# Two groups of heads at a time: kv in the off-diagonal blocks and M in four 64x64 quadrants

## The chip, the core and the metric

The kernel runs on one core of a Trainium2 chip. The core has a matrix engine (TensorE, in the profile PE, with its weight loads as PEld), VectorE (DVE), ScalarE (ACT), GpSimd (POOL), and SyncE (SP), whose queue issues all of this kernel's transfers in the order of the program. The metric is the device time of one execution in microseconds (us). Three runs of the kernel before gave 307.9, 307.93 and 309.0; their median is 307.93.

## The reference

Two blocks read the same input x (2048 rows of 640) and are mixed by a gate. Cut to what matters here:

```python
g = sigmoid((x * gate_w).sum(-1, keepdims=True))
a = A_ref(x, ...)                  # a state-space convolution, 640 channels
q, k, v = heads(x @ wqkv)          # 32 heads of 20
pq, pk = phi(q), phi(k)            # phi(t) = where(t > 0, t + 1, exp(t)) + 1e-6
kv = einsum("bhsd,bhse->bhde", pk, v)
z = einsum("bhsd->bhd", pk)
num = einsum("bhqd,bhde->bhqe", pq, kv)
den = einsum("bhqd,bhd->bhq", pq, z)[..., None] + 1e-6
b = (num / den) @ wo
return g * a + (1 - g) * b
```

kv is a 20x20 matrix for each head, so over all heads it is block diagonal, 640x640 with 32 blocks. The kernel never forms num: it multiplies kv by wo first, which gives one matrix M of 640x640, and the last stage is a product of the normalised pq with M.

## The kernel before

**Stages.** In the first stage (to about 147 us of the span) TensorE computes k for 16 row tiles and accumulates G, the product of x with phi(k), in PSUM. Since v = x @ wv, the matrix kv is Wv' G, cut to its blocks. Then comes the stage that the change is in, which mixes three things on TensorE: the q blocks (20 of them, five for each quarter of the rows; 15 matmuls of 128x128 by 512 columns each), the kv products and the M products. The last stage holds 20 final products, `fp`.

**Exactness.** Operands are split into a high and a low part (`hi` on ScalarE, `lo` on VectorE), and three matmuls give one product (`mm3`, L104 to L107). The kv and M products are instead plain fp32 matmuls, which the profile shows as two instructions for a call.

**Groups.** The 640 channels of the heads are cut into six groups of 120 (the last has 40). A group lies on the partitions in two parts of 60, from partition 0 and from 64 (`parts`, L250); the last group has one part of 40. `wo_load` (L254) loads the group's rows of wo in the same layout.

**kv of a group** (`kv_mm`, L261). For each of the five blocks b of 128 rows of G, and each part, one matmul of 128 rows by 60 weights by 60 columns; the parts write partitions 0 and 64 on of one PSUM bank of the tag `f` (three buffers). VectorE then multiplies each part with the block mask `bdm` and puts it into a diagonal block of `kvT`, a 128x128 tile in SBUF that was zeroed at the start. There are two such tiles, used in turn.

**M of a group** (`m_mm`, L271). One matmul for each half of 320 columns, with the 124x124 of `kvT` as weights and the group's rows of wo as the moving operand, into two banks of the tag `m` (two buffers). ScalarE writes the high part `Mgh`, VectorE the low part `Mgl`, for each half, and SP stores the parts to DRAM: four stores for a group, two for the last.

**Order.** The order of the stage is written out by hand in `PLAN` (L63): q is a q block, kv and m with a number are the products of that group, z and c are small steps (the gate's row, a block of the convolution), d the denominator of a quarter (`q_den`, L643), n the normalisation of a block (`q_norm`), ml the reload of M in another layout (`m_load`, L673, ten loads of 320 KB, followed by loads of u), y and f the steps of the last stage. Every engine runs its own instructions in this order; tags with a number of buffers say what waits for what. The q blocks' PSUM tag is `q` (three buffers); the denominator's product `dp` and the final products share the tag `f` with kv. The load of wo's last group waits for the buffer of group 3 and is issued behind m3 (L728).

Of the kernel before, what the change touches and what calls it, by code (L numbers as in the profile page):

```python
# [30 lines left out]
F32 = mybir.dt.float32  # L31
F32R = mybir.dt.float32r
I32 = mybir.dt.int32
AF = mybir.ActivationFunctionType
OP = mybir.AluOpType
# [4 lines left out]
P = 128  # L40
L = 2048
D = 640
NB = D // P
# [17 lines left out]


PLAN = """  # L63
q0 kv0 q0 z kv1 q0 m0 q0 m1 kv2 c q0 m2 kv3 
q1 m3 kv4 d0 q1 m4 kv5 n0 q1 n0 m5 ml n0 q1 n0 y q1 n0
q2 q2 y q2 d1 n1 f q2 n1 y f q2 n1 n1 f n1 f
q3 f q3 d2 n2 f q3 n2 f q3 n2 n2 f q3 n2 f
f d3 n3 f n3 n3 f n3 f n3 f
# [5 lines left out]
def f32(ap):  # L74
    return ap.bitcast(F32)


def body(tc, i, outT):
    nc = tc.nc
    pe, act, dve, pool, sp = nc.tensor, nc.scalar, nc.vector, nc.gpsimd, nc.sync  # L80
    outer, top, kst = ExitStack(), ExitStack(), ExitStack()

    def mk(stack, name, space=None):
        kw = {} if space is None else {"space": space}
        if space is not DRAM:
            kw["reuse_waits"] = "tile"
        return stack.enter_context(tc.tile_pool(name=name, bufs=1, **kw))
# [5 lines left out]
    pw = mk(top, "pw")  # L93
# [4 lines left out]
    def hi(dst, src):  # L98
        act.activation(dst, src, AF.Copy)  # L99

    def lo(dst, src, h, eng=None):
        (eng or dve).tensor_tensor(dst, src, f32(h), op=OP.subtract)  # L102
# [6 lines left out]
    def col(tag, n=NB, dt=F32):  # L109
        return pc.tile([P, n], dt, tag=tag, name=tag)  # L110
# [27 lines left out]
    bdm = col("bdm", HC)  # L138
    kvz = [col(f"kvT{k}", P) for k in range(2)]
# [7 lines left out]
    GT = pc.tile([P, NB, D], F32, tag="m1", name="GT")  # L147
    Wv = pc.tile([P, NB, D], F32, tag="m2", name="Wv")
    M_d = [dram.tile([D, D], F32, name=f"M_d{x}") for x in "hl"]
# [97 lines left out]
    kvs, wos = {}, {}  # L247


    def parts(gi):  # L250
        c0, n = GRP[gi]
        return [(r, c0 + o, min(HC, n - o)) for r, o in ((0, 0), (64, HC)) if o < n]
# [5 lines left out]
            m = min(64, D - c) if r == 0 else n  # L258
            sp.dma_start(w[r : r + m, :D], i["wo"][c : c + m, :])

    def kv_mm(gi):  # L261
        p = pqp.tile([P, 512], F32, tag="f", bufs=3, name="kvps")
        for b in range(NB):
            for r, c, n in parts(gi):
                pe.matmul(p[r : r + n, :n], Wv[:, b, c : c + n], GT[:, b, c : c + n],
                          start=(b == 0), stop=(b == NB - 1))
        kvT = kvs[gi] = kvz[gi % 2]
        for r, c, n in parts(gi):
            dve.tensor_tensor(kvT[r : r + n, r : r + n], p[r : r + n, :n], bdm[r : r + n, :n], op=OP.mult)

    def m_mm(gi):  # L271
        wo, kvT = wos.pop(gi), kvs.pop(gi)
        n = parts(gi)[-1][0] + parts(gi)[-1][2]
        ps = []
        for hf in range(2):
            ps.append(mbank("mps")[:n, :320])
            pe.matmul(ps[hf], kvT[:n, :n], wo[:n, hf * 320 : hf * 320 + 320], start=True, stop=True)  # L277
        h = pq.tile([P, D], F32R, tag="so", bufs=2, name="Mgh")
        l = pw.tile([P, D + 2], F32R, tag="st", bufs=3, name="Mgl")
        for hf in range(2):  # L280
            sl = slice(hf * 320, hf * 320 + 320)
            hi(h[:n, sl], ps[hf])
            lo(l[:n, sl], ps[hf], h[:n, sl])
        for v, to in ((h, M_d[0]), (l, M_d[1])):
            for r, c, m in parts(gi):
                sp.dma_start(to[c : c + m, :], f32(v[r : r + m, :D]))


    def gates():
# [5 lines left out]
    def gates_row():  # L295
        gp = mbank("gp")
        pe.transpose(gp[:NT, :P], g, ident)
        gr = pc.tile([NT, P], F32, tag="gr", name="gr")
        dve.tensor_copy(gr, gp[:NT, :P])
        sp.dma_start(g_d, gr)  # L300
        for gi in range(NG):
            gb_load(gi)
# [12 lines left out]
    def z_const():  # L315
        cp = mbank("cp")
        pe.matmul(cp[:, :2], bm, zsh, start=True, stop=False)
        pe.matmul(cp[:, :2], bm, zsl, start=False, stop=True)
        dve.tensor_scalar(ch, cp[:, :1], EPS, EPS, op0=OP.mult, op1=OP.add)
# [81 lines left out]
    def conv_out(j):  # L401
        y = conv(j)
        y_d[j] = dram.tile([P, 512], F32, name=f"y_d{j}")
        sp.dma_start(y_d[j], y)
# [190 lines left out]
    pq = mk(top, "pq")  # L595
    pqp = mk(top, "pqp", PSUM)

    def mbank(name):
        return pqp.tile([P, 512], F32, tag="m", bufs=2, name=name)

    def rem_out():
        for b0, b1 in ((0, 4), (4, NB)):
            tp = mbank("tp")
            for b in range(b0, b1):
                pe.transpose(tp[:, (b - b0) * P : (b - b0 + 1) * P], rem[:, b * P : b * P + P], ident)
            hi(GT[:, b0:b1, 512:], tp[:, : (b1 - b0) * P].rearrange("p (b s) -> p b s", s=P))
# [4 lines left out]
    def q_block(gi, b):  # L611

        qp = pqp.tile([P, 512], F32, tag="q", bufs=3, name="qp")
        w, o = (wqA, b * P) if b < 3 else (wqB, (b - 3) * P)
        for c in range(NB):
            mm3(qp, w[0][:, c, o : o + P], w[1][:, c, o : o + P], xTh[gi][:, c, :], xTl[gi][:, c, :],
                c == 0, c == NB - 1)
        if len(qe) + len(pend) == NE:
            flush()
        e = qe[gi, b] = pq.tile([P, 512], F32, tag="e", bufs=NE, name="qe")  # L620
        r = pq.tile([P, 512], F32, tag="r", bufs=2, name="qr")
        act.activation(e, qp, AF.Exp)  # L622
        act.activation(r, qp, AF.Relu)  # L623
        for h, _, v in pend:
            hi(h, v)
        dve.scalar_tensor_tensor(e, e, 1.0, r, op0=OP.min, op1=OP.add)  # L626
        if b == 0:
            a = acc[gi] = pq.tile([P, 512], F32, tag="acc", bufs=1, name="acc")
            act.activation(a, e, AF.Copy, scale=zc[:, :1])
        else:  # L630
            a = acc[gi]
            dve.scalar_tensor_tensor(a, e, zc[:, b : b + 1], a, op0=OP.mult, op1=OP.add)
        if b == NB - 1:
            ah = pq.tile([P, 512], F32R, tag="r", bufs=2, name="acch")
            al = pq.tile([P, 512], F32R, tag="accl", bufs=1, name="accl")
            hi(ah, a)
            lo(al, a, ah)
            acc[gi] = ah, al
        for h, l, v in pend:
            lo(l, v, h)  # L640
        pend.clear()

    def q_den(gi):  # L643

        dp = pqp.tile([P, 512], F32, tag="f", bufs=3, name="dp")
        ah, al = acc.pop(gi)
        pe.matmul(dp, bm, ah, start=True, stop=False)
        pe.matmul(dp, bm, al, start=False, stop=True)
        d = pq.tile([P, 512], F32, tag="d", bufs=1, name="d")
        act.activation(d, dp, AF.Identity, bias=ch)  # L650
        dve.reciprocal(d, d)
        o = pq.tile([P, 512], F32, tag="r", bufs=2, name="og")
        act.activation(o, gbs[gi], AF.Copy, bias=1.0, scale=-1.0)
        dve.tensor_tensor(d, d, o, op=OP.mult)
        rd[gi] = d

    def q_norm(gi, b):
        e = qe.pop((gi, b))
        if b == 0:
            pqT[gi] = [px.tile([P, NB, 512], F32R, tag=f"x{c}{gi}", name=f"pT{c}{gi}") for c in "hl"]  # L660
        h, l = [v[:, b, :] for v in pqT[gi]]
        dve.scalar_tensor_tensor(e, e, EPS, rd[gi], op0=OP.add, op1=OP.mult)  # L662
        flush()
        pend.append((h, l, e))
# [7 lines left out]
    m = {}  # L672
# [36 lines left out]
    for w in PLAN.split():  # L709
        what, k = w.rstrip("0123456789"), int("0" + w.lstrip("abcdefghijklmnopqrstuvwxyz"))  # L710
        if what == "q":
            q_block(*divmod(n_q, NB))
            n_q += 1
            if n_q == 1:
                rem_out()
        elif what == "z":
            z_const()
            gates_row()
        elif what == "d":
            q_den(k)  # L720
        elif what == "n":
            q_norm(*divmod(n_n, NB))
            n_n += 1
        elif what == "kv":
            kv_mm(k)
        elif what == "m":
            m_mm(k)
            if k == 3:  # L728
                wo_load(NB)
        elif what == "ml":  # L730
            m_load()
            for j in range(NS, min(NS + 3, NJ)):
                u_load(j)
        elif what == "c":
            conv_out(n_c)
            n_c += 1
            if n_c < NS:
                u_load(n_c)
        elif what == "y":
            y_block(n_y)  # L740
            n_y += 1
        elif what == "f":
            flush()
            final_mm(n_f)
            final_out(n_f)
            n_f += 1
            if n_y < NJ:
                y_block(n_y)
                n_y += 1
# [172 lines left out]
```

## Time and profile before

| | |
|---|---|
| median of three runs | 307.93 us (307.9 to 309.0) |
| profiled execution, its time | 308.53 us |
| its span, first to last instruction | 306.7 us |
| PE busy | 300.8 us, 98% of the span |
| DVE busy | 230.3 us, 75% |
| ACT busy | 118.5 us, 39% |
| POOL busy | 45.6 us, 15% |
| transfers | 45.98 MB, mean 150 GB/s |

The profile is of one execution. An engine's busy time leaves out what only waits or issues transfers. The chain of waits follows the work that ended last back from the last instruction; a piece of it has its start, its length, and the engine, tile and line. A timeline gives the instructions of one engine in order of time, equal neighbours merged (x4 is four of them), each with its start and duration; matmuls are pipelined, so the duration of one is longer than the distance to the next. A wait row reads: who waited, for whom, total us, times, longest.

### The profile page before, as it was taken

What the parts mean: (1) busy time and instruction counts of PE and PEld (TensorE: products, weight loads), DVE (VectorE), ACT (ScalarE), POOL (GpSimd) and SP (SyncE); (2) the same over time, 40 slices, a digit from 0 to 9 for tenths busy, and PEclk for the clock granted to TensorE, in tenths of its full rate; (3) what the DMA queues carried; (4) which work ended last, traced back from release to release, by engine and by line L of the source; (5) the groups of instructions that cost most, each with busy time, mean ns of one, the idle gap of its engine ahead of it and who ended that gap; (6) DMA issues with size and microseconds to landing.
All of it is one profiled execution on the core that took longest, in us unless ns stands there. A gap on an engine that the chain in (4) does not pass through costs nothing.

```text
span 306.7 us, 4494 instructions
## 1 busy us (share of the span) xinstructions
PE 300.8 (98%) x1607; PEld 259.2 (85%) x1607; DVE 230.3 (75%) x356; ACT 118.5 (39%) x249; POOL 45.6 (15%) x50
## 2 busy tenths in 40 slices
PE   8999999999999999999999999999999999999994
PEld 8998899999999999998887777888888888788884
DVE  2949976899899799937444768867684677788992
ACT  4455143453544534327335354553323223312200
POOL 3605340000000000000000000003223103241631
PEclk9999999999999999999999999999999999999999
DMA  6817285057767855380526352692315122244423
GB/s 190 296 65 223 84 245 175 35 190 226 236 161 234 255 166 174 102 268 0 158 86 219 119 170 94 196 344 79 121 50 166 42 68 68 68 139 141 134 104 108
DMA packets 28408, 45.98 MB, mean 150 GB/s; under 512 B 3771, under 2 KB 10827, under 8 KB 28383
## 3 DMA queue, kind: packets, MB, share of 16 engines
q1 hardware_dynamic: 28383, 45.66, 47.2%
q8 instruction: 14, 0.23, 0.3%
q14 instruction: 11, 0.09, 0.1%
HBM read 32.92 MB, written 12.72 MB: 149 GB/s over the span
## 4 chain that ended last, share of the span: by engine, by line
PE 94%; DVE 4%; issue 1%; ACT 0%; POOL 0%; DVEq 0%; POOLq 0%
PE qp L105 8%; PE fp L105 8%; PE fp L107 8%; PE qp L107 8%; PE qp L106 7%; PE fp L106 7%; PE k L107 6%; PE k L106 6%; PE k L105 6%; PE g L227 5%; PE g L224 5%; PE g L225 5%; PE g L430 4%; PE mps L277 2%; PE r L240 1%; PE r L238 1%
## 5 line engine op out<-in xcount | busy, mean ns | idle before, releaser
L415 POOL TENSOR_TENSOR yb<-yb,gb 128x512 f32<-128x512 f32 x20 | 28.5, 1432 | 225.7 <-DVE qe L626 162.9
L105 PE MATMUL fp<-pTh,Mh 128*128 128x512 f32 (+1 forms) x105 | 40.1, 382 | 0.6 <-DVE o L701 0.6
L107 PE MATMUL fp<-pTl,Mh 128*128 128x512 f32 (+1 forms) x105 | 40.2, 383 | 0.0
L106 PE MATMUL fp<-pTh,Ml 128*128 128x512 f32 (+1 forms) x105 | 40.0, 381 | 0.0
L626 DVE SCALAR_TENSOR_TENSOR qe<-qe,qr 128x512 f32<-128x512 f32 x20 | 14.8, 740 | 28.3 <-ACT qr L623 28.3
L224 PE MATMUL g<-ph,xh 128*128 128x512 f32 x80 | 31.6, 395 | 0.0
L225 PE MATMUL g<-ph,xl 128*128 128x512 f32 x80 | 31.5, 394 | 0.0
L199 ACT ACTIVATE e<-k 128x320 f32<-128x320 f32 x25 | 11.0, 439 | 51.5 <-PE k L107 51.5
L99 ACT ACTIVATE pTh<-qe 128x512 fp32r<-128x512 f32 x20 | 12.6, 633 | 39.3 <-DVE qe L662 39.3
L203 DVE SCALAR_TENSOR_TENSOR e<-e,r 128x320 f32<-128x320 f32 x32 | 16.2, 511 | 14.7 <-ACT r L200 14.6
L227 PE MATMUL g<-pl,xh 128*128 128x512 f32 x80 | 26.4, 394 | 0.1
L622 ACT ACTIVATE qe<-qp 128x512 f32<-128x512 f32 x20 | 12.0, 598 | 37.0 <-PE qp L107 34.6
L105 PE MATMUL qp<-xTh,wqAh 128*128 128x512 f32 x60 | 24.0, 400 | 0.0
L105 PEld LDWEIGHTS fp<-pTh,Mh 128*128 128x128 f32 x105 | 19.7, 188 | 4.9 <-DVE o L701 1.0
L107 PE MATMUL qp<-xTl,wqAh 128*128 128x512 f32 x60 | 23.6, 394 | 0.0
L106 PE MATMUL qp<-xTh,wqAl 128*128 128x512 f32 x60 | 23.6, 393 | 0.0
L106 PEld LDWEIGHTS fp<-pTh,Ml 128*128 128x128 f32 x105 | 19.7, 188 | 4.1
L107 PEld LDWEIGHTS fp<-pTl,Mh 128*128 128x128 f32 x105 | 19.8, 188 | 3.9
L395 DVE TENSOR_TENSOR_SCAN y<-y,cY,zero 128x512 f32<-128x512 f32 x16 | 20.5, 1279 | 0.9 <-ACT y L394 0.8
L102 DVE TENSOR_TENSOR pTl<-qe,pTh 128x512 fp32r<-128x512 f32 x20 | 16.0, 812 | 6.7 <-ACT pTh L99 6.3
L107 PE MATMUL k<-wkAl,xTh 128*128 128x322 f32 x60 | 19.0, 317 | 0.0
L106 PE MATMUL k<-wkAh,xTl 128*128 128x322 f32 x60 | 18.9, 315 | 0.0
(168 smaller groups left out, 725.6 us busy)
## 6 DMA issues: line engine op xcount, KB each, us to landing
xraw<-in_x SPq DMA_DIRECT2D x16, 320.0 KB, 4.8
u<-in_xT SPq DMA_DIRECT2D x20, 256.0 KB, 5.6
out_T<-o SPq DMA_DIRECT2D x19, 256.0 KB, 2.5
y_d<-y SPq DMA_DIRECT2D x16, 256.0 KB, 2.2
yb<-y_d SPq DMA_DIRECT2D x16, 256.0 KB, 3.2
xTraw<-in_xTt SPq DMA_DIRECT2D x12, 320.0 KB, 4.9
Wv<-in_wv SPq DMA_DIRECT2D x5, 320.0 KB, 6.8
Mh<-M_dh SPq DMA_DIRECT2D x5, 320.0 KB, 4.8
```

The lines of the kernel that those rows point to most:

```text
L99: act.activation(dst, src, AF.Copy)
L102: (eng or dve).tensor_tensor(dst, src, f32(h), op=OP.subtract)
L105: pe.matmul(out, ah, bh, start=start, stop=False)
L106: pe.matmul(out, al, bh, start=False, stop=False)
L107: pe.matmul(out, ah, bl, start=False, stop=stop)
L203: dve.scalar_tensor_tensor(e, e, 1.0, r[:, :n], op0=OP.min, op1=OP.add)
L224: pe.matmul(gps[b], xh[:, s], h[:, :512], start=t == 0, stop=False)
L225: pe.matmul(gps[b], xl[:, s], h[:, :512], start=False, stop=False)
L227: pe.matmul(gps[b], xh[:, b * P : b * P + P], l[:, :512], start=False, stop=t == NT - 1)
L395: dve.tensor_tensor_scan(y, y, zero.to_broadcast([P, 512]), cY[:, c], op0=OP.add, op1=OP.add)
L415: pool.tensor_tensor(ys[j], ys[j], gbs[j // NB], op=OP.mult)
L626: dve.scalar_tensor_tensor(e, e, 1.0, r, op0=OP.min, op1=OP.add)
```

## The change

Groups are taken in pairs (0 and 1, 2 and 3, 4 and 5). `kv_mm` makes the kv of both groups into one PSUM bank, the second group's in columns 64 on, with the same matmuls as before; VectorE puts the first group's two parts into the diagonal 64x64 blocks of `kvT` and the second group's into the off-diagonal ones (`out_row`: the second group's output rows change places). `m_mm` then makes one matmul for each 64x64 quadrant and half: a group's part reads 60 rows of partitions and writes 64 rows of PSUM, with its place in the array given. A half needs two banks, one for each group: the tag `m` for the first half, the tag `f` for the second. High and low parts and stores are as before, group after group, with 128 rows where it was 124. The load of wo's last group is issued behind the second pair's stores. `PLAN` has three kv and three m steps at other places, and ml follows the eighth q block where it followed the ninth.

```diff
 PLAN = """
-q0 kv0 q0 z kv1 q0 m0 q0 m1 kv2 c q0 m2 kv3 
-q1 m3 kv4 d0 q1 m4 kv5 n0 q1 n0 m5 ml n0 q1 n0 y q1 n0
+q0 kv0 q0 z q0 m0 kv1 q0 c q0 m1 kv2
+q1 d0 q1 m2 ml n0 q1 n0 n0 q1 n0 y q1 n0
...
-    def kv_mm(gi):
+    def out_row(gi, r):
+        return r if gi % 2 == 0 else 64 - r
+
+    def kv_mm(pr):
         p = pqp.tile([P, 512], F32, tag="f", bufs=3, name="kvps")
-        for b in range(NB):
-            for r, c, n in parts(gi):
-                pe.matmul(p[r : r + n, :n], Wv[:, b, c : c + n], GT[:, b, c : c + n],
-                          start=(b == 0), stop=(b == NB - 1))
-        kvT = kvs[gi] = kvz[gi % 2]
-        for r, c, n in parts(gi):
-            dve.tensor_tensor(kvT[r : r + n, r : r + n], p[r : r + n, :n], bdm[r : r + n, :n], op=OP.mult)
+        kvT = kvs[pr] = kvz[pr % 2]
+        for k, gi in enumerate((2 * pr, 2 * pr + 1)):
+            for b in range(NB):
+                for r, c, n in parts(gi):
+                    pe.matmul(p[r : r + n, k * 64 : k * 64 + n], Wv[:, b, c : c + n], GT[:, b, c : c + n],
+                              start=(b == 0), stop=(b == NB - 1))
+        for k, gi in enumerate((2 * pr, 2 * pr + 1)):
             for r, c, n in parts(gi):
+                o = out_row(gi, r)
+                dve.tensor_tensor(kvT[r : r + n, o : o + n], p[r : r + n, k * 64 : k * 64 + n], bdm[r : r + n, :n],
+                                  op=OP.mult)
 
-    def m_mm(gi):
-        wo, kvT = wos.pop(gi), kvs.pop(gi)
-        n = parts(gi)[-1][0] + parts(gi)[-1][2]
-        ps = []
-        for hf in range(2):
-            ps.append(mbank("mps")[:n, :320])
-            pe.matmul(ps[hf], kvT[:n, :n], wo[:n, hf * 320 : hf * 320 + 320], start=True, stop=True)
+    def m_mm(pr):
+        kvT = kvs.pop(pr)
+        both = 2 * pr, 2 * pr + 1
+        ps = {}
+        for hf in range(2):
+            for gi in both:
+                ps[gi, hf] = mbank("mps") if hf == 0 else pqp.tile([P, 512], F32, tag="f", bufs=3, name="mps")
+            for gi in both:
+                for r, c, n in parts(gi):
+                    o = out_row(gi, r)
+                    pe.matmul(ps[gi, hf][o : o + 64, :320], kvT[r : r + n, o : o + 64],
+                              wos[gi][r : r + n, hf * 320 : hf * 320 + 320], start=True, stop=True,
+                              tile_position=(r, o))
+        for gi in both:
+            wos.pop(gi)
+            rows = slice(0 if len(parts(gi)) == 2 else out_row(gi, 0), P)
...
+                hi(h[rows, sl], ps[gi, hf][rows, :320])
+                lo(l[rows, sl], ps[gi, hf][rows, :320], h[rows, sl])
+            for v, to in ((h, M_d[0]), (l, M_d[1])):
+                for r, c, m in parts(gi):
+                    o = out_row(gi, r)
+                    sp.dma_start(to[c : c + m, :], f32(v[o : o + m, :D]))
...
-            if k == 3:
+            if k == 1:
                 wo_load(NB)
```

More of the change, by code (lines that the diff above doesn't have):

```diff
@@ L271, in m_mm @@
-    def m_mm(gi):
-        wo, kvT = wos.pop(gi), kvs.pop(gi)
-        n = parts(gi)[-1][0] + parts(gi)[-1][2]
-        ps = []
-        for hf in range(2):
-            ps.append(mbank("mps")[:n, :320])
-            pe.matmul(ps[hf], kvT[:n, :n], wo[:n, hf * 320 : hf * 320 + 320], start=True, stop=True)
-        h = pq.tile([P, D], F32R, tag="so", bufs=2, name="Mgh")
-        l = pw.tile([P, D + 2], F32R, tag="st", bufs=3, name="Mgl")
-        for hf in range(2):
[L281 to L286, printed above, removed]
+        kvT = kvs[pr] = kvz[pr % 2]
@@ new lines, in m_mm @@
+    def m_mm(pr):
+        kvT = kvs.pop(pr)
+        both = 2 * pr, 2 * pr + 1
+        ps = {}
+        for hf in range(2):
+            for gi in both:
[9 more added lines that the diff above has]
+            rows = slice(0 if len(parts(gi)) == 2 else out_row(gi, 0), P)
+            h = pq.tile([P, D], F32R, tag="so", bufs=2, name="Mgh")
+            l = pw.tile([P, D + 2], F32R, tag="st", bufs=3, name="Mgl")
+            for hf in range(2):
+                sl = slice(hf * 320, hf * 320 + 320)
+                hi(h[rows, sl], ps[gi, hf][rows, :320])
[4 more added lines that the diff above has]
+                    sp.dma_start(to[c : c + m, :], f32(v[o : o + m, :D]))
```

## The prediction

> **What bounds the kernel now.** I read the page first (busy shares, then the chain that ended last), then the chain of waits in order of time for the stretch that the change rewrites, then the timelines of single engines there.
>
> ```profile
> PE 300.8 (98%) x1607; PEld 259.2 (85%) x1607; DVE 230.3 (75%) x356; ACT 118.5 (39%) x249; POOL 45.6 (15%) x50
> PEclk9999999999999999999999999999999999999999
> PE 94%; DVE 4%; issue 1%; ACT 0%; POOL 0%; DVEq 0%; POOLq 0%
> ```
> TensorE is busy 98% of the span at the full granted clock, and the chain runs through it for 94%. So a microsecond taken from TensorE anywhere is a microsecond of the end, as long as no other engine steps in. Two stretches, the one of the change and a late one (columns: stretch, length, then busy time and count of PE, PEld, DVE, ACT, POOL):
>
> ```profile
> 147.50:190.00 42.50, 42.50 (x277) 32.41 (x276) 24.82 (x51) 17.63 (x38) 0.00 (x0) 1.00 0.46 151
> 275.00:300.00 25.00, 25.00 (x116) 20.69 (x115) 23.37 (x26) 5.07 (x8) 10.13 (x8) 1.00 0.36 116
> ```
> In the first, VectorE has 17.7 us and ScalarE 24.9 us to spare. In the second VectorE is at 93%, but TensorE still has no gap, so time won earlier passes through.
>
> The pieces of the chain that the change touches (start, us of the chain, what):
>
> ```profile
> 166.19 1.08 PE mps L277 x4
> 167.27 0.69 PE kvps L265 x20
> 167.96 0.43 PE qp L105
> 168.39 0.23 PE qp L106
> ...
> 177.04 1.33 PE mps L277 x4
> ...
> 184.23 0.51 PE kvps L265 x10
> 184.74 0.43 PE qp L105
> ...
> 188.38 1.20 PE mps L277 x4
> 189.58 0.43 PE qp L105
> ```
> A full group's M product costs 1.08 (two calls, four instructions, each fp32 call being two), 0.27 for each pass of 320 columns. A kv costs 0.69, and the q block's matmul behind it 0.43 instead of 0.23: 0.89 in all. The last kv costs 0.51 + 0.20 = 0.71. The m3 at 177.04 has a stall of 0.25 in it. The last M product, 40 rows by 40 columns, costs 1.20 + 0.20 = 1.40, though its four passes are no longer than the others' 1.08: 0.32 goes into leaving and re-entering the full-array form.
>
> **Do small products overlap?** By 0.27/320, a pass of 60 columns is 0.0506 and one of 40 is 0.0338. The last kv (one part, ten passes one after another) is 0.338 + 0.37. A full kv, twenty passes, would be 1.01 one by one, more than the 0.89 seen; two at a time it is 0.506 + 0.38. So the two column halves do run at once, and a turn into a small form and back costs 0.32 to 0.38. How they overlap shows in two stretches of 60 ns, the first for a full kv, the second for the last one:
>
> ```profile
> 157.25 0.27 PE L265 MATMUL kvps<-GT,Wv 128*60 128x60 f32 x2
> ```
> ```profile
> 184.16 0.23 PE L265 MATMUL kvps<-GT,Wv 128*40 128x40 f32 x1
> ```
> In the full kv two matmuls start within 50 ns; on a single tile the second does not start in that time. The program's second instruction is the other pass of the same tile, so what started beside the first is the other tile's, out of program order: a tile's second pass does not hold up its neighbour. I take this for the four quadrants too.
>
> **The change, part by part.** On TensorE's path before: kv 5 x 0.89 + 0.71 = 5.16; M 4 x 1.08 + 1.33 + 1.40 = 7.05; sum 12.21.
>
> After, the same 110 kv passes, but three turns' worth of pairs; the M products become 44 passes (16, 16, 12) on four quadrants, four on each in a row, so 4 x 0.27 = 1.08 for two groups if all four run at once. Each group keeps its own bank per half.
> - kv0: 20 steps x 0.0506 + 0.38 = 1.39.
> - m0 and kv1, adjacent: 1.08 + 1.01 + one turn 0.35 + the step from 64x64 to 128x64. No row shows that step: between 0 (going on in a small form saves nothing over going on in the full one) and 0.35 (a whole turn); I take the middle, 0.17, as only one of a turn's two ends is added. 2.61.
> - m1 and kv2: 1.08 + 0.506 + 0.338 + 0.52 = 2.44.
> - m2 alone: 1.08 + 0.32 = 1.40.
>
> Sum 7.84, which is 4.37 less: 3.24 from M's passes, 0.25 from m3's stall, the rest from fewer turns. The stall goes because each kv is now two q blocks ahead of its M, where m3's was one:
>
> ```profile
> PEld mps L277 <- DVE kvT L269: 0.4, 1, 0.4
> ```
> Evacuations keep their number (12 high parts, 12 low parts, 11 masks) and their 320 columns; rows go from 124 to 128. They come eight in a row. VectorE and ScalarE hide them by the slack above, but two things queue behind. Call E the end of the fifth q block (171.45 before, where m2 began; m1 begins there after).
>
> ```profile
> 171.45 1.24 PE L277 MATMUL mps<-wo,kvT 124*124 124x320 f32 x4
> ```
> First, the denominator's product needs the bank of m1's even group, second half, and accl. VectorE did accl and the first two low parts then by:
>
> ```profile
> 175.01 0.69 DVE L102 TENSOR_TENSOR accl<-acc,acch 128x512 fp32r<-128x512 f32 x1 [0.76 <-ACT acch L99]
> 175.73 0.89 DVE L102 TENSOR_TENSOR Mgl<-mps,Mgh 124x320 fp32r<-124x320 f32 x2
> ```
> That is E + 5.17. TensorE wants the bank at E + 2.44 + a q block of 15 x 0.23 = E + 5.89. Covered by 0.7; cost 0, up to 0.5 if ScalarE is late.
>
> Second, the load of wo's last group stands in SP's queue behind all eight stores of m1, and m2 reads it. The queue before, and the landings of wo and of M's stores:
>
> ```profile
> 175.65 0.78 SPq L286 DMA_DIRECT2D M_dh<-Mgh  x2
> 176.65 0.77 SPq L286 DMA_DIRECT2D M_dl<-Mgl  x2
> 180.32 0.76 SPq L286 DMA_DIRECT2D M_dh<-Mgh  x2
> 181.18 0.80 SPq L286 DMA_DIRECT2D M_dl<-Mgl  x2
> 182.08 0.29 SPq L259 DMA_DIRECT2D wo<-in_wo  x1
> ```
> ```profile
> DMA to landing us min/median/max: 2.9/3.2/3.5
> ```
> ```profile
> DMA to landing us min/median/max: 2.1/2.3/4.2
> ```
> The first group's four stores end at E + 5.97, the second's add 1.76 (180.32 to 182.08), so the load is issued at E + 7.7 and lands 2.1 to 3.5 later, E + 9.8 to 11.2. m2 reads it at E + 2.44 + 3.45 + 0.46 (two dp) + 3.45 = E + 9.80. All four passes of that quadrant are still to come then, so lateness moves m2's end one for one: 0 to 1.4. This load is small (100 KB) and stands alone, like a store, so I take a landing of 2.6: 0.5.
>
> Third, M's reload (the ml step) moves a q block earlier. Its issues, the first product that reads it, the landings of Ml's loads, and the work that stands on VectorE ahead of it:
>
> ```profile
> 193.49 3.17 SPq L680 DMA_DIRECT2D Mh<-M_dh  x5
> 207.28 0.40 PE L105 MATMUL fp<-pTh,Mh 128*128 128x512 f32 x1
> DMA to landing us min/median/max: 5.2/5.7/6.2
> 181.27 3.35 DVE L651 RECIPROCAL d<-d 128x512 f32<-128x512 f32 x1
> ```
> E itself moves to 170.6 (4.00 spent before it, not 4.83), so m2 ends near 182.2. Before, the reload began 3.9 after the last M product; with the reciprocal and two more low parts in front it is 8.2 at worst: 190.4. Its last transfer lands 12 later (5.8 of issues, 6.2 of landing), 202.4, and the first final product, 4 us earlier too, is at about 203.4. Covered, cost 0; without the cover each microsecond counts whole.
>
> Sum: 4.37 - 0.50 = 3.87. The profiled execution, 308.53 by its time and 306.7 by its span, would be 304.7; it lies 0.6 above the median of the runs, so I apply the same 3.87 to 307.93: **304.1**.
>
> **Rivals.**
> 1. *The quadrants start in program order* (each tile's second pass blocks the next tile). Then 16 passes take nine steps of 0.27, 12 take seven: 2 x 2.43 + 1.89 = 6.75 in place of 3.24; 4.37 - 3.51 = 0.86 won: 307.1. For it: kv's total fits such an order also (11 steps instead of 10). Against: the pair at 157.25. The Trainium skill, page "TensorE: Matmul & The Clock Gate", Part 3, says of packed tiles that matmuls are a strict FIFO in start and end, with only weight loads pulled ahead; by that rule this rival is the forecast, and the two starts above disagree with it.
> 2. *Two quadrants at a time, by the bank.* The two tiles of one group write the same bank from different row halves. If they exclude each other, each group takes 2.16 per pair as it did before: 6.48, 3.24 lost, 1.13 won: 306.8. For it: no row shows two row halves at work. Against: they write different partitions, and kv's two tiles share a bank without harm. The Trainium skill, page "TensorEngine Tiling (Array Packing)", Gotcha 1, says that different row tiles cannot use one PSUM bank at the same time; no row of this trace can test it.
> 3. *The quadrants do not overlap at all* (say, each column half's output path takes one row half's stream and the two passes in turn). 44 x 0.27 = 11.88: 8.64 lost, 4.3 slower: 312.2. It decides below 11.88 / (3.24 + 4.37) = 1.6 quadrants at once. Against: kv reaches 2.
> 4. *Queues eat part of it*: wo late by the whole 1.4, the bank by 0.5 and as much again in M's reload; 4.37 - 2.4 = 2.0 won: 305.9.
>
> **Numbers.** Forecast 0.70, queues 0.07, program order 0.09, bank 0.08, no overlap 0.06. The likeliest's own range goes from 303.0 (no step, no stall: 4.37 + 0.34 = 4.7 won, 0.2 for the runs) to 305.8 (both steps a whole turn, wo late by 1.4: 2.6 won, and 0.5 for the bank). The range takes in rivals 1 and 2 up to 307.1. A measurement here can tell about 0.5%, 1.5 us, from no change: faster is the forecast and the queues, 0.77; within it rivals 1 and 2, 0.17; slower 0.06.
>
> **What would show it.** In the chain after: mps x16 at about 1.1 to 1.3 for a pair (2.2 by the bank, 2.4 by program order, 4.3 with no overlap); kvps x40 near 1.2; a wait of the last mps on the wo transfer of at most 1.4; dp without a wait on VectorE; the first fp near 203, without a wait on Mh or Ml. If the M passes overlap and the time still moves under 1.5 us, I am wrong about what follows them.

## The result, and the profile after

Six runs of the changed kernel have a median of 304.53 us (304.24 to 305.06), beside 307.91 (307.61 to 309.0) for six of the kernel before on the same chip. The ratio is 0.9897, with a 95% interval of 0.988 to 0.9914: 3.4 us less. The forecast was 304.1.

Page of the changed kernel, busy shares and the chain that ended last:

```profile
PE 296.6 (98%) x1627; PEld 255.7 (85%) x1627; DVE 230.0 (76%) x356; ACT 118.8 (39%) x249; POOL 46.9 (15%) x50
PE 87%; DVE 6%; DMA 3%; issue 1%; ACT 1%; SPq 1%; POOL 0%; DVEq 0%; ACTq 0%; POOLq 0%
```

TensorE is the bound as before. New in the chain is DMA with 3%: at one place the way back from the end leaves TensorE. The other engines' work is unchanged (VectorE 230.3 and 230.0, ScalarE 118.5 and 118.8).

TensorE's timeline after, the M and kv rows and what stands around them:

```profile
160.12 0.40 PE L107 MATMUL qp<-xTl,wqAh 128*128 128x512 f32 x1
160.44 1.31 PE L290 MATMUL mps<-wo,kvT 60*64 60x320 f32 x16
161.68 1.31 PE L272 MATMUL kvps<-GT,Wv 128*60 128x60 f32 x40
162.92 0.50 PE L105 MATMUL qp<-xTh,wqBh 128*128 128x512 f32 x1
163.27 0.39 PE L106 MATMUL qp<-xTh,wqBl 128*128 128x512 f32 x1
...
179.92 0.76 PE L290 MATMUL mps<-wo,kvT 60*64 60x320 f32 x4
181.11 1.26 PE L290 MATMUL mps<-wo,kvT 40*64 40x320 f32 x8 [0.43 <-DMA wo<-in_wo]
182.29 0.51 PE L105 MATMUL qp<-xTh,wqAh 128*128 128x512 f32 x1
```

Sixteen passes for two groups take 1.24 from their start to the start of kv. Four took 1.08 for one group before. From the end of the q block's last matmul (160.12 + 0.23) to where the first matmul behind kv would start at the full pace (0.23 ahead of the second, 163.27 - 0.23), m0 and kv1 take 2.69. A narrow stretch around the first passes shows why:

```profile
160.44 0.50 PE L290 MATMUL mps<-wo,kvT 60*64 60x320 f32 x4
```

By 160.6, that is 0.16 after the first, four of the sixteen have started, and no fifth. A pass of 320 columns takes 0.27 (1.08 for four on the full array), so no two of these four can stand one behind the other on one quadrant: each has its own. In the program the two passes of an fp32 matmul stand one behind the other on one quadrant, so the fourth quadrant's first pass is the seventh instruction, and it starts ahead of second passes that stand before it. Each bank is being written from both row halves.

m2 is the exception. Its first four passes run, then the array stops for the transfer of wo's last group. The chain of waits there, and SP's queue:

```profile
177.30 0.41 SPq L305
...
177.81 3.17 DMA wo<-in_wo
180.97 0.14 issue
181.11 1.26 PE mps L290 x8
182.37 0.43 PE qp L105
```

```profile
175.98 0.81 SPq L305 DMA_DIRECT2D M_dh<-Mgh  x2
176.89 0.82 SPq L305 DMA_DIRECT2D M_dl<-Mgl  x2
177.81 0.68 SPq L259 DMA_DIRECT2D wo<-in_wo  x1
```

The load is issued behind m1's eight stores and lands 3.17 later. The odd quadrant's first pass wants it at 179.92 and starts at 181.11, 1.19 late. The row shows 0.43 of idle only, since the even group's passes lie in the rest.

**Piece by piece** (this kernel's own pieces, a turn of the array's form included): kv0 1.45, m0 with kv1 2.69, m1 with kv2 2.51, m2 2.58; 9.23 in all, where the kernel before spent 12.21. That is 2.98 won. The timelines agree: from the first `zp` (ahead of the changed stretch) to the first final product `fp` (behind it) it is 2.96, and to the last final matmul 2.95, so nothing is lost further on:

```profile
147.45 1.17 PE L308 MATMUL zp<-ones,zacc 128*128 128x1 f32 x10
302.21 0.28 PE L107 MATMUL fp<-pTl,Mh 128*128 128x256 f32 x1
```

```profile
146.63 0.61 PE L327 MATMUL zp<-ones,zacc 128*128 128x1 f32 x5
203.50 0.40 PE L105 MATMUL fp<-pTh,Mh 128*128 128x512 f32 x1
298.44 0.28 PE L107 MATMUL fp<-pTl,Mh 128*128 128x256 f32 x1
```

The first fence is before, the second after; the first `fp` of before is at 207.28 (a row of the prediction). 207.28 - 147.45 = 59.83 and 203.50 - 146.63 = 56.87; 302.21 - 147.45 = 154.76 and 298.44 - 146.63 = 151.81. The profiled execution of before reached `zp` 0.8 later, in code that the change does not touch. The profiles of this document reach it between 146.5 and 148.2, so this lies within their spread, and it is most of why the two profiled times differ by 4.2 and the medians by 3.4.

### The profile page after: what moved, and what is told of

Read it like the earlier page. It is cut to its first block, busy times and chain, and to the rows that moved or that the text cites. A ratio compares the mean times of both kernels' runs of the same rounds, so it can differ in the third digit from the quotient of the medians.

```text
span 302.6 us, 4538 instructions
## 1 busy us (share of the span) xinstructions
PE 296.6 (98%) x1627; PEld 255.7 (85%) x1627; DVE 230.0 (76%) x356; ACT 118.8 (39%) x249; POOL 46.9 (15%) x50
## 4 chain that ended last, share of the span: by engine, by line
PE 87%; DVE 6%; DMA 3%; issue 1%; ACT 1%; SPq 1%; POOL 0%; DVEq 0%; ACTq 0%; POOLq 0%
PE fp L105 8%; PE fp L107 8%; PE fp L106 8%; PE qp L105 6%; PE qp L107 6%; PE qp L106 6%; PE k L107 6%; PE k L106 6%; PE k L105 6%; PE g L227 5%; PE g L224 5%; PE g L225 5%; PE g L449 4%; DMA M_dl<-Mgl 2%; PE r L240 1%; PE r L239 1%
## 5 line engine op out<-in xcount | busy, mean ns | idle before, releaser
L434 POOL TENSOR_TENSOR yb<-yb,gb 128x512 f32<-128x512 f32 x20 | 29.5, 1482 | 220.5 <-DMA yb<-y_d 199.2
L645 DVE SCALAR_TENSOR_TENSOR qe<-qe,qr 128x512 f32<-128x512 f32 x20 | 14.1, 704 | 23.8 <-ACT qr L642 23.8
L102 DVE TENSOR_TENSOR pTl<-qe,pTh 128x512 fp32r<-128x512 f32 x20 | 15.1, 763 | 6.8 <-ACT pTh L99 6.3
```

The lines of the kernel that those rows point to most:

```text
L434: pool.tensor_tensor(ys[j], ys[j], gbs[j // NB], op=OP.mult)
```

## The experiments

The first run of experiment 1 and experiments 2, 3 and 4 ran on one chip with 23 runs of the kernel before (median 308.28); the two later runs of experiment 1 and experiments 5 and 6 ran on another, with 11 (median 307.86). Times of different chips are compared through these.

**1. The late transfer taken away.** The load of wo's last group goes behind m1's matmuls and ahead of its stores:

```diff
+        if pr == 1:
+            wo_load(NB)
         for gi in both:
             wos.pop(gi)
...
             m_mm(k)
-            if k == 1:
-                wo_load(NB)
```

> The changed kernel with one transfer moved: the load of wo's last group is issued behind the matmuls of m1 and ahead of m1's eight stores, so about 6 us earlier. Theory (that load is the only thing m2 waits for; in the changed kernel's trace the odd quadrant's first matmul starts 1.18 us late): m2's wait on the transfer is gone, m2 falls from 2.58 to 1.40 with its turn, time 304.53 - 1.18 = 303.35. Rival (m2 is next held up by the mask on VectorE or by its banks): the wait changes its name and the time stays at 304.5.

Measured: 304.29 (302.93 to 304.81) where 303.35 was expected, ratio to before 0.9868 (0.9848 to 0.9888). The changed kernel had 0.9897, on another chip. The two intervals overlap, so it was run again beside the changed kernel:

> The changed kernel itself once more, on one chip with the three that follow, so that the early wo load can be told from it. Its wait of m2 on the wo transfer should be there again, 0.9 to 1.4 us.

> The changed kernel with the early wo load, on the same chip as the changed kernel. Theory: 1.2 us below it. Rival (the time won there is given back at a later wait): less than 0.5 below it.

Measured: 304.89 (304.29 to 305.5) for the changed kernel, ratio 0.9901 (0.9863 to 0.9938); 304.06 (303.38 to 304.95) with the early load, ratio 0.9871 (0.9833 to 0.9909). The medians differ by 0.83. Six runs of each overlap, so the times alone only lean to the theory; the traces settle it. M2 in the changed kernel here, then with the early load:

```profile
180.44 0.76 PE L290 MATMUL mps<-wo,kvT 60*64 60x320 f32 x4
181.56 1.26 PE L290 MATMUL mps<-wo,kvT 40*64 40x320 f32 x8 [0.37 <-DMA wo<-in_wo]
182.75 0.51 PE L105 MATMUL qp<-xTh,wqAh 128*128 128x512 f32 x1
```

```profile
181.57 1.23 PE mps L290 x12
```

The first takes 2.31 to the next q block, the second 1.23 as one piece of the chain. The wait cost 1.1, and no other takes its place in m2. From the first `zp` to the first final product these two profiled executions take 56.80 and 55.72, a difference of 1.08:

```profile
147.15 1.17 PE L327 MATMUL zp<-ones,zacc 128*128 128x1 f32 x10
203.95 0.40 PE L105 MATMUL fp<-pTh,Mh 128*128 128x512 f32 x1
```

```profile
148.21 0.28 PE L329 MATMUL zp<-ones,zacc 128*128 128x1 f32 x2
203.93 0.40 PE L105 MATMUL fp<-pTh,Mh 128*128 128x512 f32 x1
```

To the last final matmul they take 151.74 and 150.80, a difference of 0.94; the last section says why this longer distance is the less exact of the two.

**2. Pairs and order without the quadrants.** kv and the order as changed, each M product on the full array again. Not shown: VectorE puts the kv of each group into the diagonal blocks of a tile of its own.

```diff
             for gi in both:
-                for r, c, n in parts(gi):
-                    o = out_row(gi, r)
-                    pe.matmul(ps[gi, hf][o : o + 64, :320], kvT[r : r + n, o : o + 64],
-                              wos[gi][r : r + n, hf * 320 : hf * 320 + 320], start=True, stop=True,
-                              tile_position=(r, o))
+                n = parts(gi)[-1][0] + parts(gi)[-1][2]
+                pe.matmul(ps[gi, hf][:n, :320], kvs[gi][:n, :n], wos[gi][:n, hf * 320 : hf * 320 + 320],
+                          start=True, stop=True)
```

> The changed kernel with its order and kv in pairs, but each group's M product on the full array as before (two tiles of kv blocks, diagonal, one matmul of 124 rows by 124 weights per half and group). Theory (the overlap of the four quadrants brings most of the gain): m0 and m1 take 8 x 0.27 = 2.16 instead of 1.08 and the 0.16 step, kv1 and kv2 then pay a whole turn; m2 takes 2.16 and two turns, and no wo wait is left; 1.45 + 3.61 + 3.43 + 2.80 = 11.29 against 9.23 in the changed kernel's chain: 304.5 + 2.1 = 306.6. Rival (the gain comes from fewer turns, the new order and the stall that went): within 0.5 of 304.5.

Measured: 306.4 (306.15 to 306.76), ratio 0.9938 (0.9913 to 0.9962). Its chain:

```profile
160.41 2.15 PE mps L287 x8
162.56 1.25 PE kvps L271 x40
163.81 0.43 PE qp L105
...
181.68 2.59 PE mps L287 x8
184.28 0.43 PE qp L105
```

2.15 for two groups, twice the 1.08 of one. The pieces sum to 11.26, 2.0 more than the changed kernel's 9.23. The timeline says the same: from the first `zp` to the first final product this kernel takes 58.87, 2.00 more than the changed kernel's 56.87 and 0.96 less than the 59.83 of before:

```profile
146.53 1.17 PE L322 MATMUL zp<-ones,zacc 128*128 128x1 f32 x10
205.40 0.40 PE L105 MATMUL fp<-pTh,Mh 128*128 128x512 f32 x1
```

So in the stretch that was changed two thirds of the gain are the overlap, as the theory had it, and one third is order and pairs. The times alone do not say so: against before, order and pairs bring 1.9 by the medians (0.6% of 308.28, interval 0.4% to 0.9%), which is more than half of the changed kernel's 1.0%. Likewise the time is 2.1 above that of the early load on this chip, where the pieces say 3.2. In the profiled execution 0.6 of this lies behind the first final product, in code that the change does not touch (last section); the other 0.5 is less than the spread of the early load's runs (302.93 to 304.81).

**3. Quadrants without pairs.** The kernel before with each M product in its two diagonal quadrants:

```diff
-            ps.append(mbank("mps")[:n, :320])
-            pe.matmul(ps[hf], kvT[:n, :n], wo[:n, hf * 320 : hf * 320 + 320], start=True, stop=True)
+            p = mbank("mps")
+            ps.append(p[:n, :320])
+            for r, c, k in parts(gi):
+                m = min(64, P - r)
+                pe.matmul(p[r : r + m, :320], kvT[r : r + k, r : r + m], wo[r : r + k, hf * 320 : hf * 320 + 320],
+                          start=True, stop=True, tile_position=(r, r))
```

> The kernel before, with its own order and one group at a time, but each M product in the two diagonal 64x64 quadrants instead of one 124x124 matmul; both quadrants write the same bank from different row halves, to different partitions. Theory (two quadrants at once, so 1.08 as on the full array, and only the turns are added: 0.32 for m0, 0.16 for each of m1 to m4 that a kv follows at once): 307.9 + 0.96 = 308.9. Rival (row halves exclude each other on one bank): the passes of five groups double, 307.9 + 5.4 + 1.0 = 314.3. If quadrants alone were what helps, it would be faster than before.

Measured: 308.82 (308.08 to 309.39), ratio 1.0016 (1.0001 to 1.0031). The chain:

```profile
160.86 1.22 PE mps L280 x8
162.08 0.43 PE qp L105
...
176.87 1.22 PE mps L280 x8
178.09 0.69 PE kvps L265 x20
```

Eight passes in 1.22, where two row halves in turn would take 2.16: they write one bank at the same time. Each of m1 to m4 costs 0.14 more than the 1.08 of the full array, m0 0.34, and m3's old stall of 0.25 does not return: 0.65 by the pieces, 0.5 by the times. The 0.96 expected had left the stall out. Quadrants alone win nothing, since half of the array stands idle; the second group has to fill the off-diagonal ones.

**4. Every M matmul twice.** On the kernel with the early load:

```diff
-                    pe.matmul(ps[gi, hf][o : o + 64, :320], kvT[r : r + n, o : o + 64],
+                    for _ in range(2):
+                      pe.matmul(ps[gi, hf][o : o + 64, :320], kvT[r : r + n, o : o + 64],
...
```

> The kernel with the early wo load, with every one of the M matmuls made twice in a row (the second overwrites the first with the same numbers). Theory (four quadrants at once all through): each pair takes 4 x 0.27 = 1.08 more, 3.24 in all, 303.35 + 3.2 = 306.6, and mps x32 for a pair takes about 2.3. Two at a time it would be + 6.5 = 309.8, one at a time + 11.9 = 315.2.

Measured: 307.46 (306.92 to 308.33), 3.17 above the early load on the same chip, where 3.24 was said. A pair's piece:

```profile
160.81 2.38 PE mps L291 x32
```

Sixteen more passes cost 1.14, the length of four. So the overlap, which the rivals disputed, shows in the time and not only in a trace.

**5. Another order of the passes.** The early load, with the matmuls of a pair written out quadrant by quadrant, so that four passes in a row belong to one tile:

```diff
-            for gi in both:
-                for r, c, n in parts(gi):
-                    o = out_row(gi, r)
+        for gi in both:
+            for r, c, n in parts(gi):
+                o = out_row(gi, r)
+                for hf in range(2):
                     pe.matmul(ps[gi, hf][o : o + 64, :320], kvT[r : r + n, o : o + 64],
```

> The early wo load, with the M matmuls of a pair written out tile by tile: both halves of the first quadrant (four passes in a row on one tile), then the second, the third, the fourth. Theory (every tile has its own queue, and passes that wait for their tile hold up nobody): mps x16 stays at 1.24 and the four tiles' first passes start within 0.05 us. Rival (one pass may wait at each tile, the next one for that tile holds up all behind it): the second tile starts after two passes of the first, 0.54 later, and so on; the pair takes (6 + 4) x 0.27 = 2.7 and the time rises by 4.4. In program order throughout it would be 13 x 0.27 = 3.5 for a pair.

Measured: 304.33 in one run, within the 303.38 to 304.95 of the early load on this chip. The chain has the pair in 1.26, and a stretch from 161.30 to 161.45 shows the start:

```profile
161.47 1.26 PE mps L291 x16
```

```profile
161.40 0.52 PE L291 MATMUL mps<-wo,kvT 60*64 60x320 f32 x4
```

Four passes start within 50 ns, so on four tiles, although three more passes of the first tile stand ahead of the second tile's first one; two of them belong to a call of their own. The order in the program does not matter at this depth.

**6. All kv in one go.** The early load, a third tile of kv blocks, and

```diff
-q0 kv0 q0 z q0 m0 kv1 q0 c q0 m1 kv2
+q0 q0 kv0 kv1 kv2 z q0 q0 m0 q0 m1 c
```

> The early wo load, and all three kv pairs made in one go behind the second q block (three tiles of kv blocks), with each M pair by itself: four turns and no step from 64x64 to 128x64, instead of four turns and two steps. The small convolution step moves behind m1. By the pieces measured, kv 1.05 + 1.05 + 0.87 + 0.40 = 3.37, M 3 x 1.42 = 4.26, 7.63 against 1.45 + 2.69 + 2.51 + 1.40 = 8.05 with the early load: 0.4 below the early load. Rival (M's masks or banks now come late, m0 or m1 waits): the kvps piece is 3.2 as said, but the time is not lower.

Measured: 303.24 (302.92 to 303.95), ratio 0.9847 (0.981 to 0.9884). Six runs against the changed kernel's six on that chip (304.29 to 305.5) do not overlap; the medians differ by 1.65, 0.5%. Against the early load alone it is 0.8 by the medians, with runs that overlap, and 0.37 from the first `zp` to the first final product (202.11 - 146.76 = 55.35, and 55.72), close to the 0.4 expected:

```profile
146.76 1.17 PE L329 MATMUL zp<-ones,zacc 128*128 128x1 f32 x10
155.41 3.34 PE L272 MATMUL kvps<-GT,Wv 128*60 128x60 f32 x110
166.02 1.31 PE L290 MATMUL mps<-wo,kvT 60*64 60x320 f32 x16
202.11 0.40 PE L105 MATMUL fp<-pTh,Mh 128*128 128x512 f32 x1
```

It has the lowest median of the versions here.

## Why the prediction was right, and where it was off

**Bound.** Right: a microsecond taken from TensorE came out at the end, 2.98 by pieces and 2.95 from `zp` to the last final matmul. TensorE stops once in the last stage, for VectorE, and as long after as before (0.6).

**Overlap.** Right, and for the reason given. The 44 passes cost three times 1.08 to 1.14 (experiment 4). Rival 1, program order, falls with the four that start together and with experiment 5. Rival 2, one row half for a bank, falls with experiment 3, which has only that in it. Rival 3 falls with both. The inference from kv's two tiles to four quadrants held; the rule of program order that was weighed there does not hold for tiles of this kernel.

**Turns.** kv0 1.39 said, 1.45 measured; m0 with kv1 2.61 and 2.69; m1 with kv2 2.44 and 2.51. The step from 64x64 to 128x64, taken as 0.17 between 0 and 0.35, is 0.16: 1.24 for an M piece with kv behind it, less 1.08. The three terms together are 0.21 too small, mainly because a step of 60 columns takes 0.056 ((1.25 - 0.69) / 10, from the kv pieces of 40 and 20 passes) and not the 0.0506 worked out from passes of 320 columns.

**What queues behind.** The denominator's bank was free in time, and M's reload was hidden: no row shows a wait there. The late wo load was named, with its place in SP's queue, its issue at E + 7.7 (E is the end of the fifth q block; the load came at 177.81, with E at 169.91: E + 7.9) and its full price for m2's end. The step that was off is the size of one term: "I take a landing of 2.6". It was 3.17, within the bounds of 2.1 to 3.5, at the median of the other wo loads (3.2) and not of the stores (2.3): the reason given for 2.6, a small load that stands alone like a store, did not hold. The wait was 1.1 to 1.2, where 0.5 stood in the sum, and experiment 1 shows that it is paid at the end. With it the sum would be 3.2 instead of 3.87. Of rival 4 this one term came true, nearly whole (1.2 of 1.4); its other two were nothing.

**The base.** The sum was made against an execution whose first stage was 0.8 slower than that of the changed kernel's profile. Taking the difference off the median was the safer choice. Off the profiled time it would have given 304.66 beside the 304.36 of the changed kernel's profile, nearer than the forecast's 304.1 beside 304.53, but by luck: the slow first stage and the wait that was taken too short cancel.

## What to carry to other kernels

Where small matrices leave parts of TensorE's array empty, look first whether two independent ones can be put into the empty parts: splitting one product into its quadrants wins nothing and pays the turn (0.3, or 0.15 where another small form follows), but two in the same passes halve it. Work that comes in larger lumps also lumps its stores, and a load behind them in the one transfer queue is late by their issue time; ask for every load what is issued ahead of it. Price a landing by transfers of the same kind (here loads of wo), not by the most convenient row near it.

## What was not expected

**Two paces of the same matmul.** In the changed kernel, matmuls of 512 columns come 233 ns apart in a stretch of about 30 us behind the first final product, and again from 176 to 183 us, and 229 apart elsewhere. The profile of before has the slower pace behind its first final product too; only in experiment 2 did the profiled execution keep 229 there. The same 30 us of the changed kernel and of experiment 2 (the first count is TensorE's matmuls):

```profile
206.00:236.00 30.00, 30.00 (x130) 24.28 (x130) 20.53 (x24) 8.50 (x15) 8.88 (x7) 1.00 0.32 97
```

```profile
206.00:236.00 30.00, 30.00 (x133) 24.62 (x132) 22.07 (x25) 8.95 (x16) 9.50 (x7) 1.00 0.31 92
```

Three matmuls in 30 us are 0.6 to 0.7 us of the time, at the same granted clock (1.00). From the first to the last final matmul experiment 2 takes 94.34 and the changed kernel 94.94. What sets the pace was not tried; the one profile of experiment 2 also leaves open whether all of its runs had the faster one. It explains part of why experiment 2 came out better than its pieces.

**The spread of the part that was not changed.** With equal code in the first stage, the eight profiles of experiments and the two kernels reach `zp` between 146.5 and 148.2. The last stage spreads too. The two profiles of the kernel with the early load (experiment 1) take 55.72 each from `zp` to the first final product, but 150.00 and 150.80 to the last final matmul: the first of them lacks TensorE's one stop for VectorE in the last stage, which every other profile here has (a wait row of the second):

```profile
PE fp L105 <- DVE o L722: 0.6, 1, 0.6
```

So a gain under about 1 us is read better from the traces than from six runs, and between two points that lie close around the changed stretch, here the first `zp` and the first final product.
